# Batch 0 of an attention, gMLP and GLU kernel: the third pair's masks become two steps of their own behind two PSUM evictions

## The chip, the cores and the metric

The kernel runs on one core of a Trainium2 chip. Its time is device time in microseconds; before the change the median of three runs is 542.8 us (542.63 to 543.17). A core has a matmul engine (PE), whose weight loads are shown as PEld, two engines for elementwise work that can read the matmul accumulators in PSUM (DVE and ACT), one that cannot (POOL), and SP, which here only issues transfers. Each engine works through its own instructions in the order in which they stand, and waits on semaphores for the others.

## The reference

Three layers follow each other, for 4 batches of 576 rows.

```python
# attention, 8 heads of 64, causal window of 128
scores = scale * (q @ k.T)
scores = where((rel >= 0) & (rel < 128), scores - slope * abs(rel), -1e9)
attn = exp(scores - max);  attn = attn / (sum(attn) + 1e-09)
x = heads_side_by_side(attn @ v)                      # (576, 512)
# gated MLP that mixes along the sequence
u, v = split(gelu(x @ w_in));  v_n = layer_norm(v) * g_ln
v_s = einsum('ts,bsd->btd', w_sg, v_n) + b_sg
x = x + (u * v_s) @ w_out
# convolution and gated unit
h = relu(x @ w_in2);  out = (h * sigmoid(conv3(h))) @ w_out2
```

## The kernel before

The attention of a batch is cut into four pairs of heads. A step is a letter with numbers, and `_steps()` writes the order of all steps out as a string; `run` calls the functions named in `STEP`. For pair `b.m`: `L`, `M` load, `C` scores (PE) and masks (DVE), `E` exponentials (ACT), `N` the factors 1/sum and the scaling with them, `T` transposes of the weights (PE, into tiles `pT`, copied to `ph`), `A` the product with v (PE, tile `o`). Of the gated MLP, `V` and `U` are the two halves of the first product, `G` the product along the sequence (tile `pss`), `W` the output product (tile `pso`); `G` and `W` come in two halves of the sequence (256 and 320 columns) with four column blocks each. The attention of batch 1 is woven into the MLP of batch 0, and the string for that (`b == 0` in the loop) is what the change edits.

What a step does, where the change and the prediction touch it:

- `a_scores` (L464) issues the 46 small matmuls of a pair into five PSUM banks `sc` and then the nine masks: `masked` (L448) adds the table to a bank, takes the minimum, and frees the bank. In the trace a mask is `CUSTOM_DVE_ANT_0 t<-sc,tab` at L451 with a short read of its accumulator behind it.
- `a_norm` (L495) makes the factors `r` of a pair on DVE (L498, L499) and scales the nine blocks, on DVE or POOL (`scaled`, L242).
- `m_sg` (L840) issues 14 matmuls into a bank `pss` and evicts it on DVE with `scalar_tensor_tensor` (L856) into a tile `t1`, of which there are four. In a second visit `m_gate` follows: `t1` times `u` on POOL (L231), the high part `gh` by a copy on ACT (L222), the low part `gl` by a difference on POOL (L231).
- The network's tiles (`psu`, `psv`, `pss`, `pso`) share two PSUM banks in this stretch, the attention's (`sc`, `pT`, `o`) six: `psum(net=2, att=6)`. So the fifth `pss` needs the third one's bank, and the sixth the fourth's.
- `w_out_piece` (L373) prepares w_out in eight pieces: five DVE instructions on a tile `wa` (L324 to L331; there are two `wa`), the high part on ACT (L222) and the low part on POOL (L231), which frees `wa`. `m_wo` multiplies with both parts. The last pieces are made while `G` runs; the last two of all are `wa_1141` and `wa_1188`.
- `a_transpose` (L532) starts behind the last mask recorded so far, and for the first pair behind the last `pss` matmul recorded so far.

The order inside an engine is not the order of the string alone: a scheduler places each instruction by its own estimate of when it can start, within the dependencies; `add_manual_dep(..., follow)` adds a dependency that only orders. `book` and `pick` share elementwise work out between the engines by estimated loads.

Of the kernel before, what the change touches and what calls it, by code (L numbers as in the profile page):

```python
# [12 lines left out]
ALU = mybir.AluOpType  # L13
# [40 lines left out]
def _steps():  # L54


    def of(p):
        return f"{p // NP}.{p % NP}"

    def scores(p):  # L60
        return [f"C{of(p)}"]

    def weigh(p):
        return [f"E{of(p)}", f"N{of(p)}"]

    def back(p):
        return [f"T{of(p)}", f"A{of(p)}"]

    def halves(p):
        return [f"X{of(p)}.0", f"X{of(p)}.1"]  # L70

    def loads(p):
        return [f"L{of(p)}", f"M{of(p)}"]

    weave = lambda main, more: [
        x for i, m in enumerate(main) for x in [m] + more[i * len(more) // len(main) : (i + 1) * len(more) // len(main)]
    ]
    put_by = [f"a{i}.{c}" for i in (1, 0) for c in range(16)]
    s = """
        l0.0 k0 l1.0 k5 l2.0 l3.0 v0.0 v1.0 v2.0 v3.0 j1.0 j1.1 l0.1  # L80
        c0.0 e0.0 c1.0 e1.0 n0.0 c2.0 e2.0 t0.0 n1.0 c3.0 e3.0 l1.1 j1.2 j1.3 v0.1 i1.0 z0.0 X0.0.0 t1.0 n2.0 z1.0 X0.1.0
        l2.1 v1.1 i1.1 t2.0 n3.0 z2.0 X0.2.0 c0.1 e0.1 l3.1 j0.0 i1.2 t3.0 z3.0 X0.3.0 c1.1 e1.1 v2.1 i1.3 n0.1 c2.1 j0.1 v3.1 j0.2 t0.1 e2.1 n1.1 z0.1
        i0.0 c3.1 e3.1 j0.3 i0.1 k4 V0.0 t1.1 n2.1 z1.1 V0.1 t2.1 n3.1 z2.1 i0.2 s0.0 U0.0.0 i0.3 s0.1 t3.1 z3.1 X0.0.1 U0.0.1
        X0.1.1 U0.0.2 X0.2.1 X0.3.1
    """.split()
    for b in range(B - 1):
        p = NP * (b + 1)
        V = [f"V{b}.{j}" for j in range(5)]
        U = [[f"U{b}.{half}.{m}" for m in range(4)] for half in range(2)]
        G = [[f"G{b}.{half}.{m}" for m in range(4)] for half in range(2)]  # L90
        W = [[f"W{b}.{half}.{m}" for m in range(4)] for half in range(2)]
        if b == 0:
            uv = ["g0", "g1", V[2], "g2", "o0.0", U[0][3], "g3", "o0.1", V[4]] + loads(p) + ["g4", "o1.0"] + scores(p) + ["o1.1", V[3], "o2.0", "o2.1"]
            uv += loads(p + 1) + U[1] + ["o3.0"] + scores(p + 1) + ["o3.1"] + G[0][:2] + weigh(p) + loads(p + 2) + scores(p + 2)
        else:
            uv = V[:2] + loads(p) + scores(p) + V[2:] + loads(p + 1) + scores(p + 1) + U[0] + loads(p + 2) + U[1][:1] + scores(p + 2) + U[1][1:]
        T, A = ([f"{x}{of(p + i)}" for i in range(4)] for x in "TA")
        gw = (weigh(p) + G[0] if b else G[0][2:]) + weigh(p + 1) + G[1][:1] + loads(p + 3) + T[:1] + G[1][1:2] + W[0][:1] + A[:1] + halves(p)
        gw += weigh(p + 2) + W[0][1:2] + T[1:2] + W[0][2:] + A[1:2] + scores(p + 3) + halves(p + 1) + weigh(p + 3) + T[2:3] + G[1][2:3]
        gw += A[2:3] + halves(p + 2) + G[1][3:] + T[3:] + W[1][:1] + A[3:] + halves(p + 3) + W[1][1:]  # L100
        if b == 0:
            s += uv + gw
        else:
            now = put_by[10 * b - 10 : 10 * b]
            s += ["B1"] + weave(uv, now[:4]) + ["B0"] + weave(gw, now[4:])
    first = " ".join(s)
    n = [f"V3.{j}" for j in (0, 1, 2, 4, 3)] + [f"U3.{half}.{m}" for half in range(2) for m in range(4)]
    n += [f"G3.0.{m}" for m in range(4)] + ["G3.1.0"] + [f"W3.0.{m}" for m in range(4)]
    n += [f"G3.1.{m}" for m in range(1, 4)] + [f"W3.1.{m}" for m in range(4)]

    for m in range(4):
        n[n.index(f"U3.{m % 2}.{m // 2 + 1}")] += f" w0.{m // 2}.{m % 2}"
    n[n.index("W3.0.3")] += " y0.0"
    n[n.index("G3.1.2")] += " y0.1"
    n[n.index("W3.1.0")] += " y0.2"
    n[n.index("W3.1.1")] += " y0.3"
    s = weave(n[:-6], put_by[LATE:]) + n[-6:]
    late = [f"w1.{k}.{h}" for k in range(4) for h in range(2)]
    s = s[:-6] + weave(s[-6:], late)
    second = " ".join(["x0.0.1.2.3"] + s)  # L120
    return first, second
# [13 lines left out]
def attention_gmlp_glu_kernel(  # L135
# [21 lines left out]
    nc = tc.nc  # L157
# [10 lines left out]
    follow = mybir.DependencyInfo(mybir.DependencyClass.NoSync, mybir.DependencyReason.DATA)  # L168
    behind = mybir.DependencyInfo(mybir.DependencyClass.Sync, mybir.DependencyReason.DATA)
# [31 lines left out]
    def book(eng, ns):  # L201
        load[eng] = max(load[eng], load["pe"] - SLACK) + ns
# [62 lines left out]
    def bank(name):  # L265

        own = "all" if "all" in pools else "net" if name[:2] == "ps" or name == "idle" else "att"
        return pools[own].tile([P, 512], F32, tag="bank", name=name)
# [11 lines left out]
    gln = cpool.tile([P, NK], F32, name="gln")  # L280
    ident = cpool.tile([P, P], F32, name="ident")
    bsg = cpool.tile([P, S], F32, name="bsg")
# [117 lines left out]
    st8 = {}  # L400
# [23 lines left out]
    def weights(t, m, j, i, o=0):  # L424

        if i == 4:
            return t[:, TAIL : TAIL + 192], 8, tab[:, m, 640:832]
        nk = 192 if i else P
        part = 320 * j + (P if i else 0)
        a = o + at(i) + nk * j  # L430
        return t[:, a : a + nk], 4 * j + i, tab[:, m, part : part + nk]
# [16 lines left out]
    def masked(e, bank, table, mx):  # L448
        book("dve", 80 + width(e))
        masks[:] = [  # L450
            nc.vector.tensor_tensor_reduce(  # L451
                e, bank, table, scale=-SCALE, scalar=3e38, op0=ALU.add, op1=ALU.min, accum_out=mx
            )
        ]
# [9 lines left out]
    def a_scores(b, m):  # L464
        s = st8[b, m]
        s.update(t=ts[(b * NP + m) % NT], mx=stats[m][0], sm=stats[m][1])
        banks = {}

        def place(j, i):
            of = 4 if i == 4 else (j, i // 2)  # L470
            if of not in banks:
                banks[of] = bank("sc")
            nk = 192 if i else P
            o = 0 if i % 2 == 0 else P if i == 1 else 192
            return banks[of][:, o : o + nk]

        def mask(j, i):
            e, c, table = weights(s["t"], m, j, i)
            masked(e, place(j, i), table, s["mx"][:, c : c + 1])

        for i in range(4):
            together(scores(place(j, i), j, i, s["q"], s["k"]) for j in (1, 0))
        tc.keep_in_program_order(mm(place(0, 4), s["q"][:, 512:640], s["k"][:, 384:576], start=True, stop=True))
        for j, i in ORDER:
            mask(j, i)

    ORDER = ((1, 0), (1, 1), (0, 0), (0, 1), (1, 2), (1, 3), (0, 2), (0, 3), (1, 4))

# [6 lines left out]
    def a_norm(b, m):  # L495
        s = st8[b, m]
        r = apool.tile([P, 9], F32, tag="r", name="r", bufs=2)
        nc.vector.tensor_scalar_add(r, s["sm"], 1e-9)  # L498
        nc.vector.reciprocal(r, r)  # L499
        book("dve", 170)  # L500
        for j, i in ORDER:
            e, c, _ = weights(s["t"], m, j, i)
            scaled(e, e, r[:, c : c + 1], ON["norm"])
# [37 lines left out]
        s["waits"] = copies[-4:]  # L541
        s["ph"] = (p0, p1, pc)

    copies, masks, last_sg = [], [], []

    def product(x, half, work, waits=(), first=False, scale=False):

# [292 lines left out]
    def m_sg(b, half, d):  # L840
        sl = HALF[half]
        n = sl.stop - sl.start
        dd = slice(d * P, (d + 1) * P)
        ps = bank("pss")
        o = ps[:, :n]
        wsg = kept["wsg"]
        for c in range(4):
            hi, lo = vns[b, c]
            mm(o, hi[:, dd], wsg[0][:, c, sl], start=c == 0, stop=False)
            mm(o, hi[:, dd], wsg[1][:, c, sl], start=False, stop=False)  # L850
            mm(o, lo[:, dd], wsg[0][:, c, sl], start=False, stop=False)
        st, _ = vns[b, 4]
        mm(o, st[:, dd], wsg[0][:, 4, sl], start=False, stop=False)
        last_sg[:] = [mm(o, st[:, dd], wsg[1][:, 4, sl], start=False, stop=True)]
        t1, first = u_or_s(b, half, d)
        nc.vector.scalar_tensor_tensor(t1, o, gln[:, d : d + 1], bsg[:, sl], op0=ALU.mult, op1=ALU.add)  # L856
        book("dve", 140 + n)
        if not first:
            m_gate(b, half, d, t1)
# [25 lines left out]
    def constants(i):  # L885
# [9 lines left out]

    STEP = dict(
        B=rotations,
        k=constants, l=z_load, v=z_vload, c=z_scores, e=z_exp, n=z_norm, t=z_transpose, z=z_av, j=w_in_load, L=a_load, M=a_vload, C=a_scores, E=a_exp, N=a_norm, T=a_transpose, A=a_av,
        X=a_xsplit, V=m_v, s=m_vnorm, U=m_u, G=m_sg, W=m_wo, i=w_in_piece, g=w_sg_piece, o=w_out_piece, a=w2_piece,
    )  # L900

# [230 lines left out]
```

## Time and profile before

| | us |
|---|---|
| median of three runs | 542.8 |
| lowest, highest | 542.63, 543.17 |
| the profiled execution | 543.71 |
| its span | 541.8 |
| PE busy | 522.2 (96%) |
| DVE busy | 367.7 (68%) |
| ACT busy | 257.9 (48%) |
| POOL busy | 242.4 (45%) |

The span is the time between the first and the last instruction that the profiler shows; 1.9 us of the profiled execution lie around it. Busy shares are means over stages with different limits, so the stage of the change, from 78 to 105 us, has to be read by itself: the timeline of each engine there, and the sums over short windows. Idle time in front of a row stands in square brackets, with the instruction that ended it.

### The profile page before, as it was taken

How to read it: one execution, taken by the hardware profiler on the slowest of the kernel's cores; microseconds unless marked ns; L12 is line 12 of the kernel's file. 1: busy time of each engine (PE TensorE's matmuls, PEld its weight loads, DVE VectorE, ACT ScalarE, POOL GpSimd, SP SyncE). 2: the span in 40 equal slices, each digit the busy share in tenths (PEclk: the TensorE clock that was granted, in tenths of full speed). 3: DMA queues.
4: the chain of work that ended last, by engine and by line, in shares of the span. 5: the costliest groups of instructions: out<-in, count | busy, mean ns of one | idle time of the engine just before them, and what ended most of it. 6: DMA issues, size and time to landing. Idle time of an engine off the chain costs nothing.

```text
span 541.8 us, 11983 instructions
## 1 busy us (share of the span) xinstructions
PE 522.2 (96%) x4548; PEld 475.8 (88%) x4548; DVE 367.7 (68%) x957; ACT 257.9 (48%) x673; POOL 242.4 (45%) x385
## 2 busy tenths in 40 slices
PE   8998998999998999989999999999999999999997
PEld 6777887997998998989988989998998999999887
DVE  4999999654869775879767689687567354654300
ACT  6694586441457441376434434443554333444310
POOL 2444249451236362346443345244586545465500
PEclk9999998999998999999999999999999999999999
DMA  8974540533261766243653533901202200100011
GB/s 306 383 235 174 150 148 25 173 104 110 75 185 40 221 185 185 85 120 93 172 154 109 158 98 127 343 6 48 79 21 75 71 22 19 42 21 25 34 39 59
DMA packets 33209, 63.93 MB, mean 118 GB/s; under 512 B 3968, under 2 KB 13952, under 8 KB 33152
## 3 DMA queue, kind: packets, MB, share of 16 engines
q1 hardware_dynamic: 33008, 63.04, 36.1%
q8 instruction: 36, 0.59, 0.5%
q14 instruction: 21, 0.17, 0.1%
q10 hardware_dynamic: 144, 0.13, 0.1%
HBM read 48.47 MB, written 14.68 MB: 117 GB/s over the span
## 4 chain that ended last, share of the span: by engine, by line
PE 68%; DVE 13%; ACT 10%; POOL 4%; DMA 3%; issue 2%; SPq 0%; ACTq 0%; DVEq 0%; POOLq 0%
PE psg L213 31%; PE pso L213 8%; PE psv L213 7%; PE pss L213 6%; PE psu L213 5%; ACT t L186 4%; PE o L213 4%; PE sc L213 4%; PE pT L515 3%; DVE wa L330 1%; DMA w<-in_w_in_dram 1%; DVE t L451 1%; DVE cc L990 1%; POOL t L242 1%; DVE gg L231 1%
## 5 line engine op out<-in xcount | busy, mean ns | idle before, releaser
L213 PEld LDWEIGHTS psg<-x2g,w 128*128 128x128 f32 x768 | 103.2, 188 | 3.0 <-ACT hb L986 0.7
L213 PE MATMUL psg<-x2g,w 128*128 128x256 f32 (+1 forms) x768 | 104.9, 294 | 0.9 <-ACT hb L986 0.5
L213 PE MATMUL psg<-wout,gh 128*128 128x512 f32 (+1 forms) x272 | 80.4, 378 | 0.0
L213 PE MATMUL pss<-wsg,vn 128*128 128x256 f32 (+1 forms) x448 | 65.8, 304 | 6.3 <-DVE t L856 5.6
L213 PEld LDWEIGHTS pss<-wsg,vn 128*128 128x128 f32 x448 | 62.3, 194 | 7.6 <-DVE t L856 6.8
L186 ACT ACTIVATE t<-t,st 128x192 f32<-128x192 f32 (+1 forms) x144 | 61.9, 431 | 14.4 <-DVE st L451 14.4
L990 DVE SCALAR_TENSOR_TENSOR cc<-hb,cw,cc 128x576 f32<-128x576 f32 x32 | 27.0, 846 | 47.2 <-POOL cc L242 47.2
L213 PEld LDWEIGHTS psg<-wout,gh 128*128 128x128 f32 x272 | 49.7, 188 | 8.6
L213 PE MATMUL psu<-xg,win 128*128 128x320 f32 (+1 forms) x384 | 54.4, 298 | 1.7 <-ACT u L186 1.3
L213 PEld LDWEIGHTS psu<-xg,win 128*128 128x128 f32 x384 | 51.7, 188 | 3.4 <-ACT u L186 2.2
L213 PE MATMUL pso<-gh,wo 128*128 128x256 f32 (+1 forms) x256 | 51.4, 299 | 0.0
L213 PE MATMUL psg<-wout,gl 128*128 128x512 f32 (+1 forms) x136 | 51.2, 378 | 0.0
L213 PE MATMUL psv<-win,xg 128*128 128x512 f32 x192 | 48.2, 400 | 1.9 <-DVE wa L328 0.9
L242 POOL TENSOR_SCALAR cc<-hb,cw 128x576 f32<-128x576 f32 x32 | 27.3, 854 | 42.1 <-ACT hb L986 42.1
L213 PEld LDWEIGHTS psv<-win,xg 128*128 128x128 f32 x192 | 35.3, 188 | 10.2 <-ACT win L222 1.0
L451 DVE CUSTOM_DVE_ANT_0 t<-sc,tab 128x192 f32<-128x192 f32 (+1 forms) x144 | 40.4, 334 | 5.6 <-PE sc L213 5.6
L986 ACT ACTIVATE hb<-psg 128x576 f32<-128x576 f32 x32 | 20.6, 650 | 47.5 <-PE psg L213 46.5
L231 DVE TENSOR_TENSOR gg<-cc,hb 128x576 f32<-128x576 f32 x32 | 30.4, 949 | 17.6 <-ACT cc L186 17.4
L213 PEld LDWEIGHTS pso<-gh,wo 128*128 128x128 f32 x256 | 40.3, 188 | 0.7 <-DVE t L856 0.2
L213 PE MATMUL pso<-gl,wo 128*128 128x256 f32 (+1 forms) x128 | 36.5, 299 | 0.7 <-DVE gl L231 0.7
L231 POOL TENSOR_TENSOR t<-t,u 128x256 f32<-128x256 f32 (+1 forms) x32 | 27.1, 849 | 19.0 <-DVE t L856 18.7
L242 POOL TENSOR_SCALAR t<-t,r 128x192 f32<-128x192 f32 (+1 forms) x72 | 32.2, 463 | 4.9 <-DVE r L499 2.8
(101 smaller groups left out, 959.6 us busy)
## 6 DMA issues: line engine op xcount, KB each, us to landing
V<-in_v_dram SPq DMA_DIRECT2D x12, 704.0 KB, 4.7
x2s<-x2d SPq DMA_DIRECT2D x16, 288.0 KB, 3.0
w<-in_w_in_dram SPq DMA_DIRECT2D x8, 512.0 KB, 6.8
w<-in_w_out_dram SPq DMA_DIRECT2D x16, 256.0 KB, 3.1
w<-in_w_in_dram SPq DMA_DIRECT2D x16, 256.0 KB, 2.9
wout<-w2d SPq DMA_DIRECT2D x8, 512.0 KB, 6.0
q<-in_q_dram SPq DMA_DIRECT2D x12, 320.0 KB, 4.0
out_dram<-ot SPq DMA_DIRECT2D x15, 256.0 KB, 2.0
```

What stands on the lines that cost most here:

```text
L186: ins = nc.scalar.activation(*args, **kw)
L213: return nc.tensor.matmul(out, lhsT, rhs, start=start, stop=stop, **kw)
L231: return (nc.vector if eng == "dve" else nc.gpsimd).tensor_tensor(dst, a, b, op=op)
L242: e.tensor_scalar(dst, src, col, 1.0, op0=ALU.mult, op1=ALU.mult)
L330: nc.vector.scalar_tensor_tensor(a, high, 0xC0000000, a, op0=ALU.bitwise_and, op1=ALU.bitwise_or)
L451: nc.vector.tensor_tensor_reduce(e, bank, table, scale=-SCALE, scalar=3e38, op0=ALU.add, op1=ALU.min, accum_out=mx)
L515: ins = nc.tensor.transpose(ps[:, i * P : (i + 1) * P], src, ident)
L986: nc.scalar.activation(h[:, 1 : S + 1], ps[:, 256 : 256 + S], AF.Relu)
L990: nc.vector.scalar_tensor_tensor(cc, h[:, 0:S], cw[:, 0, c : c + 1], cc, op0=ALU.mult, op1=ALU.add)
```

## The change

The nine masks of the third pair of batch 1 (`b, m` = 1, 2) leave the step `C1.2` and become two steps, `K1.2.0` with the first four and `K1.2.1` with the last five. They stand in the string behind the third and the fourth `G` of the first half, and each mask gets an ordering dependency on the last `pss` eviction recorded so far. The first instruction of the factors of the second pair (1, 1) gets the same dependency, by then on the fourth eviction. No instruction is added or removed.

```diff
@@ -95,7 +95,7 @@
-        gw = (weigh(p) + G[0] if b else G[0][2:]) + weigh(p + 1) + G[1][:1] + ...
+        gw = (weigh(p) + G[0] if b else G[0][2:3] + [f"K{of(p + 2)}.0"] + G[0][3:] + [f"K{of(p + 2)}.1"]) + weigh(p + 1) + G[1][:1] + ...
@@ -481,8 +481,16 @@
-        for j, i in ORDER:
-            mask(j, i)
+        s["mask"] = mask
+        if (b, m) != (1, 2):
+            a_masks(b, m, 0)
+            a_masks(b, m, 1)
+
+    def a_masks(b, m, part):
+        for j, i in ORDER[4:] if part else ORDER[:4]:
+            st8[b, m]["mask"](j, i)
+            if (b, m) == (1, 2):
+                tc.add_manual_dep(masks[0].ins, last_gate[0].ins.name, follow, reason="behind pss")
@@ -495,7 +503,9 @@
-        nc.vector.tensor_scalar_add(r, s["sm"], 1e-9)
+        ins = nc.vector.tensor_scalar_add(r, s["sm"], 1e-9)
+        if (b, m) == (1, 1):
+            tc.add_manual_dep(ins.ins, last_gate[0].ins.name, follow, reason="behind pss")
@@ -853,7 +863,7 @@
-        nc.vector.scalar_tensor_tensor(t1, o, gln[:, d : d + 1], bsg[:, sl], op0=ALU.mult, op1=ALU.add)
+        last_gate[:] = [nc.vector.scalar_tensor_tensor(t1, o, gln[:, d : d + 1], bsg[:, sl], op0=ALU.mult, op1=ALU.add)]
```

`STEP` gets `K=a_masks`, and `last_gate` starts empty.

On DVE, around the third and the fourth eviction (names: `t0`, `st2` the third pair's weights and sums, `r_1357` the second pair's factors, `r_1506` the third's; `t1_1319` and `t1_1341` the third and the fourth eviction before). Before:

```order
L499 RECIPROCAL r_1357<-r_1357 128x9 [waits DVE_49]
L451 ISA t0_85,st2_90<-sc_1293,tab_78 128x192 [waits PE_49]
L451 ISA st2_90 128x1
L856 SCALAR_TENSOR_TENSOR t1_1319<-pss_1304,gln_79,bsg_81 128x256 [waits PE_49]
L324 TENSOR_SCALAR wa_1141<-wst_1139 128x256 [waits DMAHW2_49,Pool_49]
L328 TENSOR_SCALAR wa_1141<-wa_1141 128x256 [waits DVE_49]
L329 TENSOR_SCALAR wa_1141<-wa_1141 128x256 [waits DVE_49]
L330 SCALAR_TENSOR_TENSOR wa_1141<-wst_1139,wa_1141 128x256 [waits DVE_49]
L856 SCALAR_TENSOR_TENSOR t1_1341<-pss_1326,gln_79,bsg_81 128x256 [waits PE_49]
```

And now, where the third eviction is `t1_1310` and the fourth `t1_1336`:

```order
L331 SCALAR_TENSOR_TENSOR wa_1069<-wst_1067,wa_1069 128x256 [waits DVE_49]
L866 SCALAR_TENSOR_TENSOR t1_1310<-pss_1295,gln_79,bsg_81 128x256 [waits PE_49]
L451 ISA t0_85,st2_90<-sc_1267,tab_78 128x128
L451 ISA st2_90 128x1
L451 ISA t0_85,st2_90<-sc_1267,tab_78 128x192
L451 ISA st2_90 128x1
L451 ISA t0_85,st2_90<-sc_1268,tab_78 128x128
L451 ISA st2_90 128x1
L451 ISA t0_85,st2_90<-sc_1268,tab_78 128x192
L451 ISA st2_90 128x1
L324 TENSOR_SCALAR wa_1141<-wst_1139 128x256 [waits DMAHW2_49,Pool_49]
L866 SCALAR_TENSOR_TENSOR t1_1336<-pss_1321,gln_79,bsg_81 128x256 [waits PE_49]
```

The third eviction has moved ahead of all nine masks, the fourth ahead of the last five; the first instruction on `wa_1141`, which waits for POOL, now stands between four masks and the fourth eviction.

On POOL, from the gates of the last blocks of the first half to the last low part of w_out (`t2` the second pair's weights, `u_...` the other half of the gate). Before:

```order
L231 TENSOR_TENSOR wo_891<-wa_1069,wo_891 128x256 [waits Activation_49]
L231 TENSOR_TENSOR t1_1319<-t1_1319,u_843 128x256 [waits DVE_49]
L231 TENSOR_TENSOR t1_1341<-t1_1341,u_915 128x256 [waits DVE_49]
L231 TENSOR_TENSOR gl_1237<-t1_1233,gh_1236 128x256 [waits Activation_49]
L242 TENSOR_SCALAR t0_85<-t0_85,r_1506 128x128 [waits DVE_49]
L242 TENSOR_SCALAR t0_85<-t0_85,r_1506 128x192
L231 TENSOR_TENSOR wo_891<-wa_1141,wo_891 128x256 [waits Activation_49]
L242 TENSOR_SCALAR t0_85<-t0_85,r_1506 128x192 x2
L231 TENSOR_TENSOR t1_1384<-t1_1384,u_749 128x320 [waits DVE_49]
L231 TENSOR_TENSOR gl_1323<-t1_1319,gh_1322 128x256 [waits Activation_49]
L231 TENSOR_TENSOR gl_1345<-t1_1341,gh_1344 128x256 [waits Activation_49]
L231 TENSOR_TENSOR wo_891<-wa_1188,wo_891 128x256 [waits Activation_49]
```

And now:

```order
L231 TENSOR_TENSOR t1_1384<-t1_1384,u_749 128x320 [waits DVE_49]
L242 TENSOR_SCALAR t2_87<-t2_87,r_1357 128x128 [waits DVE_49]
L242 TENSOR_SCALAR t2_87<-t2_87,r_1357 128x192
L242 TENSOR_SCALAR t2_87<-t2_87,r_1357 128x128
L242 TENSOR_SCALAR t2_87<-t2_87,r_1357 128x192 x5
L231 TENSOR_TENSOR gl_1340<-t1_1336,gh_1339 128x256 [waits Activation_49]
L242 TENSOR_SCALAR t2_87<-t2_87,r_1357 128x192
L231 TENSOR_TENSOR t1_1437<-t1_1437,u_825 128x320 [waits DVE_49]
L242 TENSOR_SCALAR t0_85<-t0_85,r_1506 128x128 [waits DVE_49]
L242 TENSOR_SCALAR t0_85<-t0_85,r_1506 128x192 x3
L231 TENSOR_TENSOR wo_891<-wa_1141,wo_891 128x256 [waits Activation_49]
L231 TENSOR_TENSOR wo_891<-wa_1188,wo_891 128x256 [waits Activation_49]
```

The low part of the piece `wa_1141` has moved behind the scaling of the second and the third pair and behind the gate `t1_1437`; before, only two of the third pair's blocks stood ahead of it, and the gates and the second pair's scaling were spread otherwise.

On PE, from the last transpose of the second pair to its product with v. Before:

```order
L515 MATMUL pT_1555<-ident_80,t2_87 128x128
L213 MATMUL pso_1444<-gl_1237,wo_891 128x256 [waits Pool_49]
L213 MATMUL pso_1444<-gh_1322,wo_891 128x256 [waits Activation_49]
L213 MATMUL pso_1444<-gh_1322,wo_891 128x256
L213 MATMUL pso_1518<-gh_1214,wo_891 128x256 [waits DVE_49]
L213 MATMUL pso_1518<-gh_1214,wo_891 128x256
L213 MATMUL pso_1518<-gl_1215,wo_891 128x256
L213 MATMUL pso_1518<-gh_1236,wo_891 128x256 x2
```

And now:

```order
L525 MATMUL pT_1555<-ident_80,t2_87 128x128
L213 MATMUL pso_1444<-gh_1339,wo_891 128x256 [waits Pool_49]
L213 MATMUL pso_1444<-gl_1340,wo_891 128x256
L213 MATMUL pso_1518<-gh_1339,wo_891 128x256
L213 MATMUL pso_1518<-gl_1340,wo_891 128x256
L213 MATMUL o_1592<-ph_1556,V_1081 64x64 [waits DVE_49,Activation_49]
```

Of the 24 matmuls of the first two blocks of `pso`, 20 now stand ahead of the first pair's product `o_1461` (five before), and four are left between the second pair's transposes and `o_1592` (19 before). The first of the four multiplies with the low part of the piece `wa_1141`, and that is what its wait for POOL is for. The first pair's transposes (`pT_1397` and on) have moved from between the fifth and the sixth `pss` to behind the sixth. From `o_1592` on, PE's order is that of before up to the third layer, where a few `psg3` matmuls change places among themselves.

## Rows read from the trace of the kernel before

**Rows 1.** Waits of PE over the whole span: total, times, longest.

```profile
PE pss L213 <- DVE t L856: 5.6, 3, 2.7
```

**Rows 2.** Timeline of PE: start, length, instruction, count, idle before and releaser.

```profile
78.94 3.90 PE L213 MATMUL pss<-wsg,vn 128*128 128x256 f32 x28
85.56 3.32 PE L213 MATMUL pss<-wsg,vn 128*128 128x320 f32 x14 [2.71 <-DVE t L856]
...
90.64 2.30 PE L213 MATMUL pss<-wsg,vn 128*128 128x320 f32 x14
...
93.47 2.05 PE L213 MATMUL o<-ph,V 128*64 128x64 f32 x52
95.44 1.64 PE L515 MATMUL pT<-ident,t 128*128 128x128 f32 x13
...
99.18 2.04 PE L213 MATMUL o<-ph,V 128*64 128x64 f32 x52
```

**Rows 3.** Stretches: length, busy us PE PEld DVE ACT POOL, PEclk, DMA, GB/s.

```profile
86.70:90.00 3.30, 3.30 (x16) 3.26 (x15) 3.16 (x10) 1.11 (x5) 3.30 (x9) 0.51 0.00 0
...
84.24:99.93 15.69, 14.38 (x148) 13.93 (x150) 13.51 (x35) 8.01 (x26) 15.69 (x28) 0.89 0.14 48
...
165.00:168.40 3.40, 3.40 (x13) 3.40 (x14) 2.85 (x9) 3.40 (x17) 2.93 (x6) 0.51 0.02 5
...
99.20:150.00 50.80, 50.22 (x562) 45.58 (x565) 32.65 (x112) 19.17 (x48) 15.75 (x35) 1.00 0.35 114
```

**Rows 4.** Timeline of DVE, first pieces to sixth eviction.

```profile
73.19 0.31 DVE L328 TENSOR_SCALAR wa<-wa 128x256 f32<-128x256 f32 x1
...
84.12 0.35 DVE L451 CUSTOM_DVE_ANT_0 t<-sc,tab 128x192 f32<-128x192 f32 x1
...
84.40 0.35 DVE L451 CUSTOM_DVE_ANT_0 t<-sc,tab 128x192 f32<-128x192 f32 x1
...
85.03 0.47 DVE L856 SCALAR_TENSOR_TENSOR t<-pss,gln,bsg 128x256 f32<-128x256 f32 x1
85.67 0.82 DVE L324 TENSOR_SCALAR wa<-wst 128x256 uint32<-128x256 uint32 x1 [0.17 <-POOL wo L231]
...
87.73 0.47 DVE L856 SCALAR_TENSOR_TENSOR t<-pss,gln,bsg 128x256 f32<-128x256 f32 x1
...
88.46 0.31 DVE L498 TENSOR_SCALAR r<-st 128x9 f32<-128x9 f32 x1
...
91.13 0.54 DVE L856 SCALAR_TENSOR_TENSOR t<-pss,gln,bsg 128x320 f32<-128x320 f32 x1
...
91.99 0.71 DVE L328 TENSOR_SCALAR wa<-wa 128x256 f32<-128x256 f32 x1
```

**Rows 5.** Timeline of POOL.

```profile
84.24 0.72 POOL L231 TENSOR_TENSOR t<-t,u 128x256 f32<-128x256 f32 x1
84.92 0.72 POOL L231 TENSOR_TENSOR wo<-wa,wo 128x256 fp32r<-128x256 f32 x1
85.61 0.74 POOL L231 TENSOR_TENSOR gl<-t,gh 128x256 fp32r<-128x256 f32 x1
...
91.06 1.50 POOL L231 TENSOR_TENSOR t<-t,u 128x256 f32<-128x256 f32 x2
...
94.23 0.90 POOL L231 TENSOR_TENSOR wo<-wa,wo 128x256 fp32r<-128x256 f32 x1
...
98.38 0.74 POOL L231 TENSOR_TENSOR wo<-wa,wo 128x256 fp32r<-128x256 f32 x1
99.08 0.86 POOL L231 TENSOR_TENSOR t<-t,u 128x320 f32<-128x320 f32 x1
```

**Rows 6.** Merged chain of waits, 24 `pso` matmuls behind `o`: start, length.

```profile
101.22 2.94 PE pso L213 x24
```

**Rows 7.** Timeline of PE in later batches, two more waits for an eviction.

```profile
164.98 3.87 PE L213 MATMUL pss<-wsg,vn 128*128 128x320 f32 x14 [1.87 <-DVE t L856]
...
243.98 2.32 PE L213 MATMUL pss<-wsg,vn 128*128 128x320 f32 x14 [1.07 <-DVE t L856]
```

More of the change, by code (lines that the diff above doesn't have):

```diff
@@ L97, in _steps @@
         T, A = ([f"{x}{of(p + i)}" for i in range(4)] for x in "TA")
-        gw = (weigh(p) + G[0] if b else G[0][2:]) + weigh(p + 1) + G[1][:1] + loads(p + 3) + T[:1] + G[1][1:2] + W[0][:1] + A[:1] + halves(p)
+        gw = (weigh(p) + G[0] if b else G[0][2:3] + [f"K{of(p + 2)}.0"] + G[0][3:] + [f"K{of(p + 2)}.1"]) + weigh(p + 1) + G[1][:1] + loads(p + 3) + T[:1] + G[1][1:2] + W[0][:1] + A[:1] + halves(p)
         gw += weigh(p + 2) + W[0][1:2] + T[1:2] + W[0][2:] + A[1:2] + scores(p + 3) + halves(p + 1) + weigh(p + 3) + T[2:3] + G[1][2:3]
@@ L542, in a_transpose @@
         s["ph"] = (p0, p1, pc)
-    copies, masks, last_sg = [], [], []
+    copies, masks, last_sg, last_gate = [], [], [], []
     def product(x, half, work, waits=(), first=False, scale=False):
@@ L897, in attention_gmlp_glu_kernel @@
         B=rotations,
-        k=constants, l=z_load, v=z_vload, c=z_scores, e=z_exp, n=z_norm, t=z_transpose, z=z_av, j=w_in_load, L=a_load, M=a_vload, C=a_scores, E=a_exp, N=a_norm, T=a_transpose, A=a_av,
+        k=constants, l=z_load, v=z_vload, c=z_scores, e=z_exp, n=z_norm, t=z_transpose, z=z_av, j=w_in_load, L=a_load, M=a_vload, C=a_scores, K=a_masks, E=a_exp, N=a_norm, T=a_transpose, A=a_av,
         X=a_xsplit, V=m_v, s=m_vnorm, U=m_u, G=m_sg, W=m_wo, i=w_in_piece, g=w_sg_piece, o=w_out_piece, a=w2_piece,
```

## The prediction

> **What bounds the kernel now.** PE is busy 96% of the span, so time is lost where PE waits or runs at its lower clock. The view of PE's waits comes first: its largest single cause is a `pss` matmul waiting for an eviction, 5.6 us in three waits [rows 1]. PE's own timeline shows the longest of them in the stretch of the change: the fifth `pss` starts at 85.56, after 2.71 us of nothing [rows 2]. [...] At half speed 3.3 us of clock cost about 1.65 us. So some 4.4 us look recoverable.
>
> The DVE timeline says why: the third eviction runs at 85.03, though its last matmul lies at about 81, because nine masks stand before it; the fourth follows at 87.73 [rows 4]. But POOL, 45% busy over the span by the table, is busy without a gap from 84.24 to 99.93, 15.69 of 15.69 us [rows 3]. Its queue holds the gates, the low parts, the scaling and the last w_out pieces, nearly all of which PE needs [rows 5]. In this stretch POOL is as tight as PE, and that is the point on which I forecast.
>
> **The change part by part.** No instruction goes or comes, so the sum is one of waits. I use the profiled execution (543.71 us, a span of 541.8 and 1.9 around it), take the instant when `o_1592` starts, 99.18 before [rows 2], and ask when it starts now. PE's work behind it is that of before, with only 0.58 us idle from 99.20 to 150 [rows 3], so a shift there should reach the end. The reordered `psg3` matmuls of the third layer I count as nothing: PE has other matmuls in between.
>
> *Third eviction.* It needs only the end of the L331 that stood behind four masks and now stands before them; it moves from 85.03 to about 82.5. The fifth `pss` starts near 83.05 instead of 85.56: the 2.71 us go, and with them the cause of that slow stretch.
>
> *Fourth eviction.* It moves less than the string suggests, because L324 on `wa_1141` stands ahead of it and waits for the POOL piece that starts at 84.92 and takes 0.72 [rows 5]. As before, L324 starts at 85.67 and takes 0.82 [rows 4]; the eviction then ends at 85.67 + 0.82 + 0.47 = 86.96. PE, done with the fifth `pss` at 83.05 + 2.30 = 85.35, waits 1.65 us.
>
> *Fifth eviction.* Between 85.67 and its end DVE has the eviction (0.47), five masks at 0.28 (the pitch of 84.12 to 84.40), the second pair's `r` (0.31), five pieces of w_out (L324, L328, L324, L329, L328) and itself (0.54) [rows 4]; 2.72 us plus the pieces. A piece takes 0.31 when POOL rests (73.19) and 0.71 to 0.82 beside it: 91.99 + 0.71 ends at 92.70, 0.14 after the two POOL products that end at 92.56, and 85.67 + 0.82 ends at 86.49, 0.14 after the one that ends at 86.35 [rows 4, 5]. So beside two-input work on POOL such a piece gets through about when POOL finishes one. Low bound 85.67 + 2.72 + 5 × 0.31 = 89.9; high bound with 5 × 0.82, 92.5. POOL now does seven such products in a row, to 84.24 + 0.68 + 0.69 + 5 × 0.74 and a little = 90.1 (pitches and lengths of [rows 5]). The first three pieces are therefore held (ends near 86.5, 88.0, 88.7), the three masks and `r` bring 89.8, the fourth piece waits until 90.2, the fifth runs free, and the eviction ends at about 91.05. I take that.
>
> [...]
>
> *POOL's queue.* From the gate at 84.24 to `wa_1141`'s low part POOL has exactly what it had from 84.24 to 99.94 before (three gates of 256, two of 320, four low parts, 13 scaled blocks, four w_out pieces), less one w_out piece of 0.74, which comes last now. With no idle time the piece ends at 99.94 − 0.74 = 99.2 [rows 5]; before, it ended at 94.23 + 0.90 = 95.1. The gate behind the fifth eviction waits for it: POOL is free at 90.1, so 91.05 adds 0.95 us and the piece ends at 100.15. Bounds: no idle time, 99.2; 2.4 us, 101.6.
>
> *PE behind it.* The first of the four `pso` matmuls in front of `o_1592` waits for that piece. PE is there earlier: from 83.05 it has 2 × 2.30, 1.64 for transposes, 20 `pso` matmuls at 2.94 / 24 = 0.12 [rows 6], 2.05 and 1.64 again [rows 2], 12.4 us, with the wait of 1.65 at 97.1, and with 1 us for the first pair's copies, which now stand on ACT behind the gate of the fifth `pss`, at 98.1. Even another slow stretch of 1.65 us would bring it there at about 99.8, hidden. So `o_1592` starts at 100.15 + 4 × 0.12 + 0.05 = 100.7, against 99.18: **+1.5 us**, with bounds of +0.5 and +2.9. The other way to it, transposes of the second pair, copies and product, took 99.18 − 95.44 = 3.7 us at most; POOL ends the scaling that starts it ahead of the piece by a gate (0.86), four scaled blocks and the piece itself (0.74), so it comes out close to the same.
>
> The profiled execution would become 545.2; as it lies 0.9 over the median, I forecast 542.8 + 1.5 = 544.3 for the median. What was late at the third eviction is late again at a POOL piece fifteen microseconds on.
>
> **Rivals.**
>
> 1. *POOL does not idle, or part is given back.* The floor of +0.5 alone, up to +1.0, or a shift that later waits for evictions take up: 542.8 to 543.8, say 543.4. For it: DVE pieces at 0.31 do not delay the fifth eviction. Against: seven POOL products stand beside them.
> 2. *A slow clock in front of `o_1592`.* Slower by a mechanism of its own: PE idles about 2 us (98.1 to 100.2) before the four `pso` matmuls. A wait of 1.87 us was followed by 14 matmuls in 3.87 us, one of 1.07 by the same 14 in 2.32 [rows 7], and the clock after the first was 0.51 for 3.4 us [rows 3]. If PE's last idle piece here reaches about 1.7 us in one go, the slow stretch comes behind it, where nothing hides it: 1.5 + 1.6 = 3.1, 545.9. Against: an earlier slow stretch or a longer wait for the copies shortens that idle time.
> 3. *The gain arrives.* If POOL's queue were shorter than I read it, or PE's wait for the piece ended early, PE would save 2.71 + 1.65 less the 1.65 us wait at the sixth `pss` and about 1 us for copies: −1.7, 541.1. For it: both losses are in the trace. Against: POOL has no gap to start earlier, and the order puts the piece at its end.
> 4. *It does not do what it says.* The fourth eviction is held by L324, so half of the intent fails; if delays elsewhere cancel the rest, the time stays at 542.8.
>
> **How the numbers follow.** Differences below 0.2% (1.1 us) cannot be told from none here. Forecast (+1.1 to +2.4): 0.40. Rival 1: 0.18, rival 4: 0.12, both within 0.2%. Rival 2: 0.20, slower. Rival 3: 0.10, faster. That gives faster 0.10, same 0.30, slower 0.60. The range from 542.3 to 546.2 leaves out rival 3 and the top of rival 2, about 0.15 in all.
>
> **What would show it.** In the changed profile: the wait of 2.71 us before the fifth `pss` is gone and the clock is 1.00 from 86 to 87; the fourth eviction starts at about 86.5, right behind L324, and the sixth `pss` waits over 1 us for it; POOL idles about 1 us before the fifth block's gate; the piece of w_out ends at 99.2 to 101; PE idles before the four `pso` matmuls on POOL; `o_1592` starts at 99.7 to 102. I am wrong if the fourth eviction comes before 85.5, if POOL's queue ends before 99, if PE waits for something else before `o_1592`, or if `o_1592` is late and the end is not.

## The result and the profile after

Ten runs of the changed kernel have a median of 546.61 us (543.82 to 547.77), ten of the kernel before on the same chip 543.17 (542.63 to 545.32). The ratio over all runs is 1.0051 (the medians alone would give 1.0063), with a 95% interval of [1.003, 1.0071]: slower by 0.5%, which on the 542.8 us of the forecast is 545.6 (544.4 to 546.7). The forecast was 544.3, its slower neighbour (rival 2) 545.9. The profiled execution took 546.72 with a span of 544.9.

Traces of two executions begin differently (at a product of the first layer, 20.62 before, the changed kernel is already 0.58 behind, at 21.20), so places are compared from the second pair of `pss` (the reference below), which starts at 78.94 before [rows 2] and at 79.50 in the changed kernel: 0.56 is taken off below. PE's timeline of the changed kernel (start, length, instruction, count, idle before and releaser):

```profile
79.50 3.91 PE L213 MATMUL pss<-wsg,vn 128*128 128x256 f32 x28
83.79 2.33 PE L213 MATMUL pss<-wsg,vn 128*128 128x320 f32 x14 [0.38 <-DVE t L866]
87.51 2.32 PE L213 MATMUL pss<-wsg,vn 128*128 128x320 f32 x14 [1.39 <-DVE t L866]
...
93.75 0.51 PE L213 MATMUL pso<-gh,wo 128*128 128x256 f32 x2 [0.84 <-DVE t L866]
...
97.47 1.64 PE L525 MATMUL pT<-ident,t 128*128 128x128 f32 x13 [0.22 <-POOL t L242]
...
100.88 0.38 PE L213 MATMUL pso<-gh,wo 128*128 128x256 f32 x1 [1.77 <-POOL wo L231]
...
101.55 3.40 PE L213 MATMUL o<-ph,V 128*64 128x64 f32 x52
...
109.70 4.41 PE L213 MATMUL pss<-wsg,vn 128*128 128x320 f32 x28
```

The 2.71 us before the fifth `pss` [rows 2] are 0.38 now. In their place stand 1.39 before the sixth, 0.84 before earlier `pso` matmuls and 1.77 before the four `pso` matmuls in front of `o_1592`, and the product `o_1592` behind them (101.55) takes 3.40 instead of 2.04. It starts 22.05 behind the reference, 20.24 before: +1.81. The seventh and eighth `pss`, at 109.70, are 3.37 later than before (row below, read the same way): 1.56 more have come from the slow product and the matmuls behind it. At the end of the two traces 2.5 us are left (from the second pair on, 465.4 us against 462.9).

```profile
105.77 4.41 PE L213 MATMUL pss<-wsg,vn 128*128 128x320 f32 x28
```

The chain of waits of the changed kernel, from the piece of POOL that L324 waits for to `o_1592`, in pieces (start, length, what):

```profile
85.53 0.71 POOL wo L231
...
86.26 0.80 DVE wa L324
...
90.97 0.47 DVE t L866
...
91.52 1.05 POOL t L231
92.57 3.74 POOL t L242 x8
...
97.01 0.40 POOL t L242
97.42 0.83 POOL t L231
98.25 1.89 POOL t L242 x4
100.14 0.70 POOL wo L231
...
```

From 86.26 to 91.44 the chain lies on DVE: it begins with L324, which waits for POOL, goes through masks, w_out pieces and factors, and ends with the fifth eviction, for which POOL waits. From 91.52 on it is POOL alone, and the piece of w_out comes last, behind nine blocks of the second pair, a gate and four blocks of the third. Before, PE was busy for 14.38 of 15.69 us here, at a granted clock of 0.89 [rows 3]. The sums of the changed kernel for the same stretch and for its two slow ones (length, busy us of PE, PEld, DVE, ACT, POOL, PEclk, DMA, GB/s):

```profile
102.00:105.30 3.30, 3.30 (x47) 3.05 (x43) 1.01 (x3) 1.09 (x3) 0.00 (x0) 0.50 0.25 84
84.80:100.50 15.70, 11.45 (x121) 10.21 (x120) 12.50 (x37) 9.14 (x31) 14.73 (x26) 1.00 0.14 43
170.20:173.60 3.40, 3.40 (x17) 3.36 (x16) 3.11 (x10) 3.40 (x18) 2.02 (x6) 0.50 0.02 5
```

PE now idles 4.25 us of that stretch, at full clock; POOL idles 0.97. The slow stretch of 86.70 [rows 3] is gone, and one has come at 102.00, behind `o_1592`'s start, where PE has nothing to wait for. The other, of batch 1, is in both traces.

The single runs fit this. A slow stretch lowers a run's mean granted clock by 0.003 (the trace before has two, of 3.30 and 3.40 us at 0.51 [rows 3], and a mean of 0.994), so the mean tells how many a run had, but not where. The two of the changed kernel at 0.999 (none) took 543.82, the six at 0.994 (two) a median of 546.9: 1.54 for each. Of the kernel before, over all comparisons of this study, the 11 runs with none have a median of 541.83 (541.34 to 543.03), the 43 with one 543.2, the 25 with two 543.0. So at no slow stretch the change costs about 2.0, near the 1.81 of the trace, though by two runs only; and the two stretches before cost 1.2 together, while both now count. One of them was therefore nearly free on average. That it was the one of 86.70 is likely, but not shown: in the trace before, PE waits for nothing from 85.56 to 99.93.

### The profile page after: what moved, and what is told of

The parts are those of the page before. It is cut to its first block, busy times and chain, and to the rows that moved or that the text cites. A ratio compares the mean times of both kernels' runs of the same rounds, so it can differ in the third digit from the quotient of the medians.

```text
span 544.9 us, 11983 instructions
## 1 busy us (share of the span) xinstructions
PE 524.3 (96%) x4548; PEld 477.4 (88%) x4548; DVE 367.9 (68%) x957; ACT 258.2 (47%) x673; POOL 243.0 (45%) x385
## 4 chain that ended last, share of the span: by engine, by line
PE 63%; DVE 13%; ACT 10%; POOL 6%; DMA 4%; issue 2%; SPq 0%; ACTq 0%; DVEq 0%
PE psg L213 30%; PE psv L213 7%; PE pso L213 6%; PE psu L213 6%; ACT t L186 4%; PE pss L213 4%; PE o L213 4%; PE sc L213 3%; POOL t L242 3%; PE pT L525 2%; DMA w<-in_w_in_dram 2%; DVE wa L330 1%; DVE wa L328 1%; DVE cc L1000 1%; DVE wa L329 1%
## 5 line engine op out<-in xcount | busy, mean ns | idle before, releaser
L213 PE MATMUL pss<-wsg,vn 128*128 128x256 f32 (+1 forms) x448 | 64.0, 299 | 5.6 <-DVE t L866 4.7
L213 PEld LDWEIGHTS pss<-wsg,vn 128*128 128x128 f32 x448 | 60.5, 189 | 7.2 <-DVE t L866 6.1
```

The lines of the kernel that those rows point to most:

```text
L213: return nc.tensor.matmul(out, lhsT, rhs, start=start, stop=stop, **kw)
```

## The experiments

P is the theory of the prediction: POOL's piece of w_out comes too late for PE, and the idle time before it brings the slow clock. D says that the evictions on DVE decide. Each kernel was compared with the kernel before on its own chip. "Shift" is the start of `o_1592` less that of the second `pss` pair, against 20.24 before; "at the next `pss`" is the same for the seventh `pss`, against 26.83.

| kernel | shift of `o_1592` | at the next `pss` | median, before | ratio, 95% |
|---|---|---|---|---|
| the change | +1.81 | +3.37 | 546.61, 543.17 | 1.0051 [1.003, 1.0071] |
| e1 | +1.18 | +1.17 | 543.63, 542.45 | 1.002 [1.0005, 1.0034] |
| e2 | +1.51 | +1.51 | 542.38, 542.45 | 1.0005 [0.9995, 1.0016] |
| e4 | +5.48 | +5.48 | 547.47, 542.45 | 1.0089 [1.0073, 1.0104] |
| e7 | +1.81 | +1.79 | 546.46, 542.45 | 1.0066 [1.0044, 1.0088] |
| e6 | -0.02 | -0.02 | 542.55, 543.0 | 0.9992 [0.9977, 1.0006] |
| e9 | +1.28 | +1.26 | 543.76, 543.0 | 1.0027 [1.0007, 1.0047] |
| e10 | +1.86 | +1.86 | 545.6, 543.0 | 1.0038 [1.0019, 1.0056] |
| e11 | +0.33 | +0.33 | 543.85, 543.0 | 1.0017 [0.9995, 1.0038] |
| e12 | -0.07 | +0.02 | 543.39, 543.25 | 1.001 [0.9999, 1.0022] |
| e13 | -0.61 | +0.43 | 543.5, 543.79 | 0.999 [0.9974, 1.0006] |

**e1: POOL's order alone.**

```diff
...
+            if (b, m) == (1, 2) and eng == "pool":
+                tc.add_manual_dep(ins.ins, last_wo[0], follow, reason="behind w_out")
...
```

The lines left out hand on POOL's instruction and the name of the last low part.

> The changed kernel, but POOL makes the low parts of both last w_out pieces ahead of the scaling of the third pair; nothing else moves on any engine. Theory P (POOL's queue puts the low part of wa_1141 late, PE idles 1.77 us for it, and the slow stretch comes behind that idle time): the piece ends about 1.9 us earlier, near 99 (on the trace of the changed kernel, where it started at 100.11), PE's wait for it and the stretch of low clock behind o_1592 go, o_1592 starts when the copies of the second pair's transposes end, about 100.7 there; time about 546.6 - 0.85 - 1.6 = 544.2, or 544 to 545 if only one of the two goes. Rival D (the loss comes from the fourth eviction held by L324 and from the copies, POOL's piece only happens to end last): o_1592 starts within 0.4 us of 101.5, the time stays at 546 or above.

POOL's timeline, then PE's, of e1:

```profile
97.68 1.44 POOL L231 TENSOR_TENSOR wo<-wa,wo 128x256 fp32r<-128x256 f32 x2
```

```profile
87.01 2.32 PE L213 MATMUL pss<-wsg,vn 128*128 128x320 f32 x14 [1.41 <-DVE t L869]
...
96.95 1.64 PE L528 MATMUL pT<-ident,t 128*128 128x128 f32 x13 [0.22 <-POOL t L242]
...
100.42 2.04 PE L213 MATMUL o<-ph,V 128*64 128x64 f32 x52 [1.20 <-DVE ph L224]
```

The wait for POOL's piece and the slow product are gone, six of the 12 runs have no slow stretch (two of ten in the changed kernel), and the time falls to 0.2% above before: P. D's forecast of no gain falls, since the 1.41 us before the sixth `pss` are still there. But of the 1.81 only 0.63 are gained. `o_1592` now waits for the copies of the second pair's transposes, which stand at 96.95 behind POOL's scaling. The six runs with no slow stretch have a median of 543.2, 1.4 over those of the kernel before, near the shift.

**e6: the same order in the kernel before** (the diff of e1, on the kernel before).

> The kernel before, with the same POOL order as in e1_wout_first: both last low parts of w_out ahead of the scaling of the third pair. Theory P (POOL's piece is late only because the change moved it): in the kernel before the piece ended at 95.1 and nothing waited for it, so the time stays within 0.2% of before and o_1592 within 0.3 us of 99.2. Rival (POOL's order is a limit of the kernel before as well, and e1 gained for a reason that has nothing to do with the change): faster by 1 us or more.

No difference, as P has it: POOL's order costs only where the change has put the piece late.

**e9: the hold of the factors alone**, without the masks.

```diff
...
+        if (b, m) == (1, 1):
+            tc.add_manual_dep(ins.ins, last_gate[0].ins.name, follow, reason="behind pss")
...
```

> The kernel before with only the hold of the second pair's factors behind the fourth eviction; the masks stay where they were, so the third eviction is late and the wait of 2.7 us before the fifth pss stays. Theory P: POOL now scales the second pair behind the two gates and their low parts, its last block ends near 95 instead of 90.4, the second pair's transposes follow at 95.5 to 96.5 and o_1592 3.5 to 3.7 us behind them, 99.2 to 100.2: 0 to 1 us over before, and the slow stretch stays where it costs little. Rival (the hold of the factors is where the whole loss comes from): o_1592 at 101 or later, 2 us or more over before.

POOL's timeline, then PE's, of e9, and a row of POOL before:

```profile
93.17 0.75 POOL L231 TENSOR_TENSOR wo<-wa,wo 128x256 fp32r<-128x256 f32 x1
93.89 2.13 POOL L242 TENSOR_SCALAR t<-t,r 128x192 f32<-128x192 f32 x4
```

```profile
96.08 1.64 PE L517 MATMUL pT<-ident,t 128*128 128x128 f32 x13 [0.32 <-POOL t L242]
...
100.40 2.05 PE L213 MATMUL o<-ph,V 128*64 128x64 f32 x52 [1.07 <-DVE ph L224]
```

```profile
86.33 4.06 POOL L242 TENSOR_SCALAR t<-t,r 128x128 f32<-128x128 f32 x9
```

The hold alone gives +1.28 (a little over what P expected), by the path on which e1 was left: POOL's last block of the second pair ends at 96.02, where it was done at 90.39 before (86.33 + 4.06), and transposes, copies and product follow. The last two copies stand besides on DVE behind an `xg` instruction that waits 0.73 us for ACT. The piece of w_out ends at 93.92 and no one waits for it.

**e4: the masks alone**, the change without that hold.

> The masks part of the change alone: the second pair's factors are not held, so DVE makes them and POOL scales the second pair before the gates, and the low part of wa_1141 stands behind two, not four, blocks of the third pair and ahead of the sixth gate. Theory P: the piece ends 2 to 3 us earlier, o_1592 no longer waits for it and starts at 99.5 to 100.5; the last low part of the gates, gl_1340, is late instead and is needed by pso matmuls next; time 543 to 544.5. Rival D: the fourth eviction is still behind L324 and the sixth pss still waits over 1 us, so the time stays at 545 or above.

DVE's timeline, POOL's and PE's of e4, and the sums of its slow stretch (columns as above):

```profile
92.29 2.98 DVE L242 TENSOR_SCALAR t<-t,r 128x128 f32<-128x128 f32 x4
...
95.66 0.53 DVE L864 SCALAR_TENSOR_TENSOR t<-pss,gln,bsg 128x320 f32<-128x320 f32 x1
```

```profile
92.90 2.25 POOL L231 TENSOR_TENSOR t<-t,u 128x256 f32<-128x256 f32 x3
```

```profile
87.68 2.32 PE L213 MATMUL pss<-wsg,vn 128*128 128x320 f32 x14 [0.78 <-DVE t L864]
...
96.25 0.80 PE L213 MATMUL pso<-gh,wo 128*128 128x256 f32 x2 [2.87 <-DVE t L864]
```

```profile
95.80:102.50 6.70, 6.25 (x63) 5.75 (x64) 1.73 (x3) 0.87 (x3) 5.34 (x9) 0.50 0.01 2
```

This is 3 us over what P expected, and though D's number covers it, its reason does not: the sixth `pss` waits 0.78 us, not over 1. The sixth eviction stands on DVE behind the scaling of the third pair, whose blocks take 0.75 each beside POOL's products; `pso` waits 2.87 us for its bank, and 6.7 us at half clock follow. The masks, moved by themselves, make DVE late; the hold of the factors, by itself, makes POOL late (e9). Together they cost less than the masks alone.

**e2: the fourth eviction ahead of the w_out piece** (the steps `o3.0` and `o3.1` behind the last five masks, L324 held behind the eviction).

```diff
-... G[0][3:] + [f"K{of(p + 2)}.1"]) + weigh(p + 1) ...
+... G[0][3:] + [f"K{of(p + 2)}.1", "o3.0", "o3.1"]) + weigh(p + 1) ...
...
```

> The changed kernel, but the w_out piece wa_1141 is begun behind the fourth eviction instead of ahead of it. Both theories: the fourth eviction runs at about 84.7 instead of 86.98 and the wait of 1.39 us before the sixth pss goes. Rival D: that is where the time was lost, so o_1592 comes about 1.4 us earlier and the time falls to about 545 or lower. Theory P: PE's wait only moves to the four pso matmuls before o_1592, which still stand behind POOL's piece; POOL's piece comes a little earlier since POOL idles less before the fifth block's gate (at most 0.97 us), so o_1592 comes 0 to 1 us earlier, with more idle time in front of it and the slow stretch behind it; time 545.5 to 547.

Timelines of e2, PE's, then a row of DVE's and one of POOL's:

```profile
82.47 4.38 PE L213 MATMUL pss<-wsg,vn 128*128 128x320 f32 x28 [0.38 <-DVE t L868]
...
91.39 0.50 PE L213 MATMUL pso<-gh,wo 128*128 128x256 f32 x2 [2.19 <-DVE t L868]
...
93.42 3.14 PE L213 MATMUL o<-ph,V 128*64 128x64 f32 x52
96.49 1.64 PE L527 MATMUL pT<-ident,t 128*128 128x128 f32 x13
...
99.93 2.05 PE L213 MATMUL o<-ph,V 128*64 128x64 f32 x52 [1.33 <-DVE ph L224]
```

```profile
97.18 1.29 DVE L224 COPY ph<-pT 128x512 f32<-128x512 f32 x2 [2.59 <-PE pT L527]
```

```profile
94.30 0.90 POOL L231 TENSOR_TENSOR wo<-wa,wo 128x256 fp32r<-128x256 f32 x1
```

The wait before the sixth `pss` is gone, as both theories said, and comes back as 2.19 us for the sixth eviction. `o_1592` gains 0.30 only. That lies in P's range, but not for P's reason: POOL's piece now stands ahead of the gate and of the third pair's blocks and ends at 95.20, and PE no longer waits for it. Nor is the slow stretch free here, though a wait follows it: the first pair's product takes 3.14 instead of 2.04, the transposes stand right behind it, and the copies that `o_1592` waits for stand behind them. At full clock, if nothing else held it, `o_1592` would be about 1.1 earlier still (an estimate from these two lengths), 1.4 in all, which is what D expected. So e2 moved the eviction and the piece at once and doesn't decide between P and D. The total is that of before, by the ratio 1.2 us better than the shift says, and P's time is missed. Ten of the 12 runs had one slow stretch and two had two; the profiled one has none in batch 1, and why is open, so e2 is no proof of a gain.

**e7: filler in the idle time.**

```diff
...
+        for _ in range(fill):
+            ins = nc.tensor.matmul(o, tab[:, 0, :128], tab[:, 0, :512], start=True, stop=True, skip_group_check=True)
...
```

Seven such matmuls (`fill`) stand behind the second pair's transposes.

> The changed kernel with seven more matmuls of 512 columns between the second pair's transposes and the four pso matmuls, where PE idles 1.77 us; what they write is overwritten. They take about 1.5 us and nothing waits for them longer than PE does already. Theory that the stretch of low clock (102.0 to 105.4 in the changed kernel's trace, about 1.6 us of loss) is set off by the idle time in front of it: o_1592 starts within 0.3 us of where it did, the granted clock stays at 1.00 behind it, the time is 545.0, 1.6 lower. Rival (the low clock comes by the time or by something else, not by this idle time): the stretch stays, and the time is 546.6 or up to 0.3 above.

PE's timeline of e7, and the sums behind `o_1592`'s start:

```profile
98.47 1.67 PE L561 MATMUL o<-tab 128*128 128x512 bf16 x7
100.42 0.39 PE L213 MATMUL pso<-gh,wo 128*128 128x256 f32 x1 [0.27 <-POOL wo L231]
...
101.09 2.05 PE L213 MATMUL o<-ph,V 128*64 128x64 f32 x52
```

```profile
101.10:104.40 3.30, 3.30 (x64) 3.19 (x64) 1.73 (x5) 1.21 (x3) 0.80 (x2) 1.00 0.47 104
```

In this place the theory holds: the seven matmuls fill 1.67 us (expected: about 1.5), `o_1592` starts where it did (+1.81), takes 2.05 instead of 3.40, and the next `pss` is 1.58 earlier than in the changed kernel. Its time did not fall (546.46). The trace of the profiled run shows where the gain went:

```profile
320.63 0.39 PE L213 MATMUL pso<-gl,wo 128*128 128x256 f32 x1 [1.81 <-DVE gl L231]
```

Up to there PE is 2.0 us earlier than in the changed kernel's trace (each on its own clock), but the `gl` that it needs from DVE ends at 320.58 (319.63 + 0.95), hardly earlier than there (319.81 + 0.97 = 320.78), where PE came just in time for it; the chain to it goes through a load of w_in (2.54 us from 311.70). So PE waits 1.81 us, and a slow stretch follows at 322 (six `pso` matmuls take 1.48 us from 323.12 on), where the changed kernel's trace has none (1.09 for such six, from 322.68). Three other runs had no slow stretch at all and took 544.19, 545.65 and 548.1; that spread stays open. The gain is shown in its place and not in the total.

**e10 and e11: the w_out pieces behind the sixth eviction, with POOL's two orders.** e10 moves `o3.0` and `o3.1` behind the sixth `pss`, with L324 held as in e2; e11 adds the lines of e1.

> The changed kernel, but both last w_out pieces are begun on DVE behind the sixth eviction, so that neither the fourth nor the sixth eviction stands behind them; POOL makes their low parts last, behind the third pair's scaling and the sixth gate. Theory P: the waits of PE for the fourth and the sixth eviction (1.39 and 0.84 us) go, but PE then waits for POOL's low part before o_1592, which ends at about 98.5 on e2's clock (where o_1592 started at 99.93): o_1592 about 99, with over 1 us of idle time in front of it; time 542 to 544. Rival D (evictions alone decide): o_1592 at 97 to 97.5, time 540 to 541.

> e10_wout_after_sixth with POOL's order changed alone: the low parts of both w_out pieces ahead of the third pair's scaling (six blocks, about 2.6 us). Theory P: the piece ends about 2.6 us earlier, near 96, PE no longer waits for POOL, o_1592 starts when the second pair's copies end, near 97 to 97.5 on e2's clock, 1 us earlier than in the kernel before; with no idle time over 1.5 us before it the slow stretch becomes rare in this place; time 540.5 to 542, the first version ahead of both kernels. Rival D: no difference to e10.

Timelines of e10 (DVE, PE), then of e11:

```profile
86.84 3.35 DVE L508 TENSOR_SCALAR r<-st 128x9 f32<-128x9 f32 x1
...
96.31 3.29 PE L213 MATMUL o<-ph,V 128*64 128x64 f32 x52 [2.28 <-issue]
```

```profile
85.76 0.56 DVE L509 TENSOR_SCALAR r<-st 128x9 f32<-128x9 f32 x1
...
93.34 3.63 PE L213 MATMUL o<-ph,V 128*64 128x64 f32 x52 [1.45 <-issue]
```

`o_1592` differs by 1.53 us (+1.86 to +0.33), but the pair says nothing on POOL's piece. The difference is there before that piece is needed: the first pair's product starts 16.38 behind the reference in e10 and 14.49 in e11, and from that product to `o_1592` PE shows no wait in either trace (the piece ends at 100.23 in e10 and at 96.63 in e11, each before PE comes to it). It comes from DVE: the first instruction of the second pair's factors starts 6.91 behind the reference in both, and takes 0.56 in e11 but 3.35 in e10, until POOL's row of products ends at 90.16. The fifth eviction and all that follows on DVE stand behind it. Whether other runs of e10 had this is not on record, and the intervals of the two ratios overlap. Both starts are 1.3 to 1.8 us later than I expected, and both times lie above P's ranges; in e11 a slow clock, which stretches the first product from 2.04 to 3.63, would account for most of it.

**e12 and e13: the next waits.** e12 holds the third pair's factors behind the sixth eviction as well; e13 puts the last piece, `wa_1188`, behind the second pair's transposes, and the second block of `pso` behind it.

> e11_sixth_and_wout_first with one more hold: the factors of the third pair stand behind the sixth eviction on DVE, where in e11 they waited for ACT's exponentials until 89.52 with the eviction (90.14) behind them. Theory P (PE is now held only by that eviction and by the first pair's copies, POOL's pieces are early): the sixth eviction comes at about 88.3 on e11's clock, PE's wait of 0.81 us goes, the copies of the first pair start over 1 us earlier, the product o in front of the second pair's transposes starts at about 91.5 to 92.5 instead of 93.34 and at full clock, o_1592 at 97 to 98 instead of 99.42; time 540.5 to 542, ahead of the kernel before by 0.2% or more. Rival (POOL's scaling of the second pair, which ends at 93.04, or its low part of w_out, which started at 95.89, holds o_1592 at 98.5 or later): no more than 0.2% from before.

> e12_factors3_after_sixth with the last w_out piece (wa_1188) begun behind the second pair's transposes, so that their copies on DVE no longer stand behind its five instructions. In e12 the transposes started at 94.53, the piece of POOL that the pso matmuls need ended at 97.18, but o_1592 waited 1.83 us more, until 99.80, for copies that stood behind that last piece. Theory P: o_1592 starts between 98 and 98.7 on e12's clock, 1.2 to 1.8 us earlier; the second block of pso then waits for the last piece up to 1 us later on, so 0.5 to 1.5 us of it reach the end: 542 to 543 where e12 took 543.4. Rival (the last piece is late for pso by as much as the copies are early, or another entry of the same queues takes their place): no difference to e12.

PE's timeline of e12, then of e13:

```profile
99.80 2.04 PE L213 MATMUL o<-ph,V 128*64 128x64 f32 x52 [1.83 <-DVE ph L224]
```

```profile
98.19 2.04 PE L213 MATMUL o<-ph,V 128*64 128x64 f32 x52 [1.15 <-DVE ph L224]
```

In e12 the steps came as expected up to the transposes; then their copies stood on DVE behind the last w_out piece, and `o_1592` came at 99.0 on e11's clock, where the rival has it. In e13 it is 0.54 earlier than in e12, under half of what I expected, and 0.61 earlier than in the kernel before. The next `pss` is 0.43 later than before: it starts 7.63 behind `o_1592`, against 6.68 in e12. That the last piece, now made at 101.26, is the reason fits the order, but no wait in the trace names it. Neither is measurably faster than the kernel before.

## Why the prediction was right, and where it was wrong

- *Third eviction*: forecast 82.5, measured 83.26 - 0.56 = 82.70. The wait went, and with it the slow stretch: the forecast's half speed, 1.65 us for 3.3, is the clock of 0.51 from 86.70 to 90.00 [rows 3], where the changed kernel has 1.00 from 84.80 to 100.50.
- *Fourth eviction*: held by L324 until "about 86.5"; 86.98 - 0.56 = 86.42. PE's wait, forecast 1.65, was 1.39.
- *Fifth eviction*: forecast end 91.05; 90.89 + 0.54 - 0.56 = 90.87. POOL idled 0.97 for it (forecast 0.95). One sum on the way is written wrongly: seven products, with 5 × 0.74, give 89.3 and not 90.1. There are eight, which end at 90.55 - 0.56 = 89.99, so the 90.1 that the rest uses holds. That POOL's products hold DVE's short pieces was the working behind this number, and it fits the rows of DVE's timeline of the changed kernel: L324 takes 0.83 beside products, L329 0.28 while POOL waits.

```profile
88.43 0.83 DVE L324 TENSOR_SCALAR wa<-wst 128x256 uint32<-128x256 uint32 x1
...
90.49 0.28 DVE L329 TENSOR_SCALAR wa<-wa 128x256 uint32<-128x256 uint32 x1
```

- *POOL's queue*: piece forecast to end at 100.15; 100.14 + 0.70 - 0.56 = 100.28. Then `o_1592`: forecast 100.7, measured 100.99: the piece ended 0.13 later, and the four `pso` matmuls take 0.67 and not 0.53.
- *The term that was mis-sized* is the last: the forecast let +1.5 reach the end at full clock. The slow stretch behind the idle time adds 1.56, which I had as rival 2 at a chance of 0.20. Its condition was an idle time of about 1.7 us in one piece, an estimate between the 1.07 and the 1.87 us of [rows 7], and my own walk gave 2.05 (98.1 to 100.15); 1.77 came, and the slow stretch behind it. By the walk's own numbers rival 2 was the forecast. I had marked it down for delays that might shorten the idle time; PE did arrive 0.45 later, and it was not enough. No run shows 1.7 us, or the 1.5 us of e11's expectation, as a limit: behind 1.45 us the product of e11 took 3.63 us, behind 1.83 us that of e12 took 2.04. The measured 545.6 is nearer to rival 2's 545.9 than to the forecast's 544.3; it lies in the range because the range took in most of rival 2.
- *The step that was incomplete*: the loss was put on the piece, with "the other way to it" named as close to the same. e9 and e1 show that other way to be worth +1.2 to +1.3 by itself; the piece adds 0.6 on top, and the slow stretch comes with it. Whether the lower bound of +0.5, for a POOL that never idles, could have been reached is not shown: POOL waits about 1 us for DVE in both runs (0.96 in e1, 1.08 in e9).
- *Rival 3* (the gain arrives) is out: PE's 2.71 us went and 1.39 + 0.84 (for the sixth eviction, at the `pso` bank) + 1.77 came. *Rival 4* is half true: the fourth eviction did not get free, but freeing it (e2) moves `o_1592` by 0.30, or about 1.4 if the slow clock there is taken off. What share of the loss is the fourth eviction's stays open, since e2 moved POOL's piece as well.

## What to carry to other kernels

Where an engine off the critical path is busy without a gap in just the stretch that one changes, walk its queue in the new order before counting the wait that goes: here that walk came within 0.3 us of the trace. Where two engines share one tight stretch, a wait that is pushed out comes back at the next entry that stands in the wrong place: the reorderings moved it, and none is measurably faster than the kernel before. Follow each trace's chain before reading two runs as a test of one edit: e2 moved more than its edit says, and e10 lost its time on another engine. And ask of a slow clock whether the work that it slows lies on the chain to the last wait: in e2 it does, although PE waits behind it.

## What the runs showed of the hardware

The slow clock does not follow from the idle time alone. The fifth `pss` of batch 1 waits 1.86 or 1.87 us in all twelve traces; before, the 14 matmuls behind it took 3.87 [rows 7]. In the changed kernel and in e1, from PE's timelines:

```profile
168.82 3.01 PE L213 MATMUL pss<-wsg,vn 128*128 128x320 f32 x14 [1.87 <-DVE t L866]
```

```profile
166.12 2.32 PE L213 MATMUL pss<-wsg,vn 128*128 128x320 f32 x14 [1.87 <-DVE t L869]
```

Three lengths, 3.87, 3.01 and 2.32, for the same idle time: the low clock set in early, later, or not at all. Before, the granted clock was 0.51 from 165.00 on [rows 3], just behind the start of the 14 matmuls (164.98); in the changed kernel it was 1.00 from their start (168.82) to 170.00 and 0.50 from 170.20 on; in e1 they took about what the same 14 took before at a clock of 1.00, 2.30 from 90.64 on [rows 2]. What sets the moment is not shown. So one execution of a kernel doesn't tell what such an idle time costs; the single runs help, by their mean clocks: in the changed kernel they go from 543.82 with no slow stretch to 547.77 with two.

A short instruction of DVE lasted six times as long in one trace as in another: the 128x9 instruction of the factors took 0.56 us in e11 and 3.35 in e10, begun at the same place. In e10 it ended at 90.19, with POOL's row of products (90.16), so POOL most likely held it; why it got through in e11 is open.
